# Pooled attention and two token layers on one core: engine queues from a planned task list, first two token blocks interleaved

## The chip, the cores and the metric
One core of a Trainium2 chip. The metric is device time in microseconds for one execution of the whole program, median of the runs; one execution was also profiled. Engines: TensorE (PE, with its weight loads PEld), VectorE (DVE), ScalarE (ACT), GpSimd (POOL), and SyncE (SP), whose queue issues all DMAs here. An engine runs its queue in the order in which the kernel wrote it.

## The reference
Attention over keys and values that are averaged in groups of 8, then two layers over all 4608 tokens. All inputs are float32.

```python
k_p = k.reshape(B, H, Sp, 8, D).mean(axis=3)         # B, H, S, D = 8, 8, 576, 64; Sp = 72
v_p = v.reshape(B, H, Sp, 8, D).mean(axis=3)
attn = softmax(q @ k_p.T / sqrt(D)) ; x = attn @ v_p # x: 4608 tokens x 512
h = x @ w_in                                         # 2048 inner columns
P = a[0] + a[1]*h + a[2]*h*h + a[3]*h*h*h
Q = 1.0 + abs(b[0])*abs(h) + abs(b[1])*h*h
x = (P / (Q + 1e-6)) @ w_out
out = (sigmoid(x @ w_gate) * (x @ w_val)) @ w_out2   # 1536 inner columns
```

## The kernel before
Float32 products are made of three matmuls each, of high and low parts (`mm3`, lines 500 to 502). The weights come as float32 and are taken apart once: two activations (lines 92, 94), a shift on VectorE (line 100) and an add on GpSimd (line 102), then a high part (line 117) and a low part (line 118, on VectorE for w_in, on GpSimd for w_out).

The tokens go through attention and the first layer in 9 blocks of 512 tokens. The inner columns of the first layer are 16 pieces of 128. A **step** n is one block's one piece: n = 16 x block + piece, 144 steps. `g1` makes the hidden tile h (12 matmuls of 512 columns) in one of four PSUM banks handed out in turn (`new_ps`); `rational1` to `rational3` (lines 541 to 560) make the rational function on ScalarE and VectorE, with line 560 as h's last reader; `split_g` takes the result apart (lines 525, 528); and `g2`, three steps later, adds the piece's product with w_out into four accumulator banks, which `store` evicts and writes to DRAM (x2d) once a block is done.

Between the steps stands the attention of the next block, tile by tile (tiles of up to 128 tokens of one batch; 5 tiles in odd blocks, 4 in even ones): `scores` (sc, line 369; maxima and differences at 380, 382), `exponential` (388), `normalise` (395 to 399, the last on GpSimd), `a_transpose` (pta at 406, aT at 410), `attend` (psx at 421, xs at 426 and 427). Its PSUM tiles come from the same four banks in turn. Keys are pooled on VectorE (`pool_k`, 318) and copied into the block-diagonal kbd (`place_k`, 327); values are pooled on GpSimd (`pool_v`, 335, 336), and those of the first batch partly on VectorE (`pool_v0`, 348 to 351).

The order is written by hand: `put` gives each attention task a step and a rank, and the loop over n calls, in a fixed order, g1, the attention's tasks of this step, the rational function, g2 and `weights_a` or `background`. The first block's attention, and the first weights, run ahead of step 0. During steps 0 to 15 `weights_a` converts the first layer's weights, one piece of w_in and of w_out a step; pieces 5 to 15 of w_out are written back to DRAM (wod) and read again for each later block (`wo_stream`). From step 16 to 127 `background` converts the weights of the second layer. From step 128 the second layer's first inputs and weights are loaded. The second layer (`gate`, `value`, `h2`, from 974 us) runs on its own order.

Of the kernel before, what the change touches and what calls it, by code (L numbers as in the profile page):

```python
# [33 lines left out]

@with_exitstack
def attention_moe_glu_kernel(ctx: ExitStack, tc: tile.TileContext, q, k, v, w_in, w_out, ca, cb, w_gate, w_val, w_out2, out):
# [13 lines left out]
    NTT = TB // P  # L50
# [10 lines left out]
    LAG = 3  # L61
# [5 lines left out]
    xs_p = ctx.enter_context(tc.tile_pool(name="xs", bufs=2))  # L67
    rot = ctx.enter_context(tc.tile_pool(name="rot", bufs=1))
    g_p = ctx.enter_context(tc.tile_pool(name="g", bufs=3))
    ps_h = ctx.enter_context(tc.tile_pool(name="ps_h", bufs=4, space=PSUM))  # L70
    ps_a = ctx.enter_context(tc.tile_pool(name="ps_a", bufs=1, space=PSUM))

    def new_ps(name):
        return ps_h.tile([P, 512], F32, tag="h", name=name)

    def new_tmp(name, tag="m", bufs=3):
        return rot.tile([P, 512], F32, tag=tag, name=name, bufs=bufs)

    x2d = [dram.tile([P, NJ, TB], F32, name=f"x2d{i}", tag=f"x2d{i}") for i in range(NB)]

    def conv1a(*raws):

        for raw in raws:
            hw, lw = raw[:, :, 1], raw[:, :, 0]

            nc.scalar.activation(hw.bitcast(F32), hw.bitcast(F32), AF.Prelu, scale=2.0 ** -112, alpha=2.0 ** 32)

            nc.scalar.activation(lw, lw.bitcast(U32), AF.Copy, scale=2.0 ** -29)

    def conv1b(*raws):

        ws = [(raw[:, :, 1], raw[:, :, 0]) for raw in raws]
        for hw, lw in ws:
            nc.vector.tensor_scalar(out=hw, in0=hw, scalar1=3, scalar2=None, op0=ALU.logical_shift_left)  # L100
        for hw, lw in ws:
            nc.gpsimd.tensor_tensor(out=hw, in0=hw, in1=lw, op=ALU.add)

    between = []

    def conv1(*raws):
        conv1a(*raws)
        between.append(lambda: conv1b(*raws))

    def gap():  # L110
        for f in between:
            f()
        between.clear()

    def conv2(raw, wh, wl, eng=nc.gpsimd):
        t = raw[:, :, 1].bitcast(F32)
        nc.scalar.activation(wh, t, AF.Copy)
        eng.tensor_tensor(out=wl, in0=t, in1=wh.bitcast(F32), op=ALU.subtract)

    def load_raw(raw, src, by_cols):  # L120
        if by_cols:
            nc.sync.dma_start(raw.rearrange("p (c f) w -> p c (f w)", f=P), src.rearrange("(c p) x -> p c x", p=P))
        else:
            nc.sync.dma_start(raw.rearrange("p f w -> p (f w)"), src)

    def slot(tag, dtype, name, pool=None):
        shape = [P, 2, 4 * P] if dtype is F32R else [P, 4 * P, 2]
        return (pool or wp).tile(shape, dtype, tag=tag, name=name)

    wod = {f: dram.tile([P, 8 * P], F32, name=f"wod{f}", tag=f"wod{f}") for f in range(FS, NF1)}  # L130


    w2d = [dram.tile([P, 14, 4 * P], F32, name=f"w2d{s_}", tag=f"w2d{s_}") for s_ in range(NS)]
    wo2d = [dram.tile([P, 8 * P], F32, name=f"wo2d{f}", tag=f"wo2d{f}") for f in range(NF2)]


    wi, wo, wi_raw, wo_raw = {}, {}, {}, {}

    def wi_src(f):
        return w_in[:, 2 * f * P:2 * (f + 1) * P]  # L140

    def wi_load(f):
        wi_raw[f] = slot(f"wi{f + 1}", I32, "wiraw") if f + 1 < NF1 else slot("st5", I32, "wiraw", stage)
        load_raw(wi_raw[f], wi_src(f), True)

    def wi_conv1(f):
        conv1(wi_raw[f])

    def wi_conv2(f):
        wi[f] = slot(f"wi{f}", F32R, "wi")  # L150
        conv2(wi_raw.pop(f), wi[f][:, 0], wi[f][:, 1], nc.vector)
# [739 lines left out]
```

## Time and profile before
| | us |
|---|---|
| median of 3 runs | 1812.47 (1809.62 to 1812.76) |
| profiled execution, span | 1813.5 |
| TensorE busy | 1761.6 |
| VectorE busy | 1104.0 |
| ScalarE busy | 975.8 |
| GpSimd busy | 801.3 |

The span is the time from the first to the last instruction of the profiled execution; it lies 1 us above the median of the runs. Busy time is the time in which at least one instruction of an engine ran. Matmuls are pipelined, so a busy TensorE may still be one that runs at the lower of its two clocks: the granted clock stands beside it, as a share of full speed.

### The profile page before, as it was taken

How to read it: one execution, taken by the hardware profiler on the slowest of the kernel's cores; microseconds unless marked ns; L12 is line 12 of the kernel's file. 1: busy time of each engine (PE TensorE's matmuls, PEld its weight loads, DVE VectorE, ACT ScalarE, POOL GpSimd, SP SyncE). 2: the span in 40 equal slices, each digit the busy share in tenths (PEclk: the TensorE clock that was granted, in tenths of full speed). 3: DMA queues.
4: the chain of work that ended last, by engine and by line, in shares of the span. 5: the costliest groups of instructions: out<-in, count | busy, mean ns of one | idle time of the engine just before them, and what ended most of it. 6: DMA issues, size and time to landing. Idle time of an engine off the chain costs nothing. (4 is left out here: it accounts for less than half of the span.)

```text
span 1813.5 us, 25319 instructions
## 1 busy us (share of the span) xinstructions
PE 1761.6 (97%) x9056; PEld 1525.1 (84%) x9056; DVE 1104.0 (61%) x1788; ACT 975.8 (54%) x1763; POOL 801.3 (44%) x787
## 2 busy tenths in 40 slices
PE   6699999999999999999999999999999999999999
PEld 5578787788878887788878998998998998998997
DVE  6898887878888888888776333333433333433341
ACT  5998877687877777877875222222222222222221
POOL 3766554563555536634442324324324334334231
PEclk8899999999999999999999999999999999999999
DMA  8564444543544454425465753763763763763660
GB/s 258 169 202 144 151 156 145 195 152 131 202 170 156 139 193 161 168 100 176 167 221 197 236 181 128 236 182 125 240 186 120 240 197 109 238 201 106 206 198 36
DMA packets 128209, 313.60 MB, mean 173 GB/s; under 512 B 16596, under 2 KB 48340, under 8 KB 128084
## 3 DMA queue, kind: packets, MB, share of 16 engines
q1 hardware_dynamic: 128084, 311.99, 52.8%
q8 instruction: 72, 1.18, 0.3%
q14 instruction: 53, 0.43, 0.1%
HBM read 257.95 MB, written 52.95 MB: 171 GB/s over the span
## 5 line engine op out<-in xcount | busy, mean ns | idle before, releaser
L674 DVE TENSOR_TENSOR t<-h,t 128x384 f32<-128x384 f32 x360 | 200.8, 558 | 388.0 <-ACT t L682 273.0
L528 POOL TENSOR_TENSOR g<-y,g 128x512 fp32r<-128x512 f32 x144 | 187.2, 1300 | 283.8 <-ACT g L525 216.6
L727 POOL TENSOR_TENSOR t<-t 128x384 f32<-128x384 f32 x72 | 84.4, 1172 | 449.0 <-issue 253.4
L500 PE MATMUL acc<-g,wo 128*128 128x512 f32 x576 | 233.7, 406 | 0.0
L500 PE MATMUL h<-xs,wi 128*128 128x512 f32 x576 | 231.3, 402 | 2.2 <-DVE xs L427 2.0
L502 PE MATMUL acc<-g,wo 128*128 128x512 f32 x576 | 226.8, 394 | 1.3 <-POOL g L528 1.3
L501 PE MATMUL h<-xs,wi 128*128 128x512 f32 x576 | 226.5, 393 | 0.0
L502 PE MATMUL h<-xs,wi 128*128 128x512 f32 x576 | 226.4, 393 | 0.0
L501 PE MATMUL acc<-g,wo 128*128 128x512 f32 x576 | 226.0, 392 | 0.0
L502 PE MATMUL h<-xS,wq 128*128 128x384 f32 x576 | 193.4, 336 | 0.0
L500 PE MATMUL h<-xS,wq 128*128 128x384 f32 x576 | 193.2, 335 | 0.0
L501 PE MATMUL h<-xS,wq 128*128 128x384 f32 x576 | 193.0, 335 | 0.0
L541 ACT ACTIVATE u<-h,coef 128x512 f32<-128x512 f32 x144 | 98.2, 682 | 104.7 <-PE h L502 104.4
L558 DVE SCALAR_TENSOR_TENSOR y<-y,coef,h 128x512 f32<-128x512 f32 x144 | 107.4, 746 | 75.2 <-ACT h L554 73.0
L543 DVE SCALAR_TENSOR_TENSOR u<-u,coef,h 128x512 f32<-128x512 f32 x144 | 106.4, 739 | 70.9 <-ACT y L542 70.3
L500 PE MATMUL h<-xA,wq 128*128 128x384 f32 x432 | 149.4, 346 | 0.1
L502 PE MATMUL h<-xA,wq 128*128 128x384 f32 x432 | 144.9, 335 | 0.0
L501 PE MATMUL h<-xA,wq 128*128 128x384 f32 x432 | 144.9, 335 | 0.0
L500 PEld LDWEIGHTS h<-xs,wi 128*128 128x128 f32 x576 | 109.7, 191 | 26.8 <-DVE xs L427 3.0
L500 PEld LDWEIGHTS acc<-g,wo 128*128 128x128 f32 x576 | 109.0, 189 | 26.5 <-issue 4.6
L502 PEld LDWEIGHTS acc<-g,wo 128*128 128x128 f32 x576 | 108.9, 189 | 25.6 <-POOL g L528 1.7
L502 PEld LDWEIGHTS h<-xs,wi 128*128 128x128 f32 x576 | 109.3, 190 | 23.8 <-DVE xs L427 0.2
(115 smaller groups left out, 4041.2 us busy)
## 6 DMA issues: line engine op xcount, KB each, us to landing
wq<-w2d SPq DMA_DIRECT2D x252, 512.0 KB
wo<-wod SPq DMA_DIRECT2D x88, 512.0 KB
w2d<-wq SPq DMA_DIRECT2D x36, 512.0 KB
x2d<-o SPq DMA_DIRECT2D x36, 256.0 KB
out_dram<-o SPq DMA_DIRECT2D x36, 256.0 KB
raw<-in_k_dram SPq DMA_DIRECT2D x32, 256.0 KB
raw<-in_q_dram SPq DMA_DIRECT2D x32, 256.0 KB
wiraw<-in_moe_w_in_dram SPq DMA_DIRECT2D x16, 512.0 KB
```

What stands on the lines that cost most here:

```text
L500: nc.tensor.matmul(out_, wl, xh, start=start, stop=False, skip_group_check=on)
L501: nc.tensor.matmul(out_, wh, xh, start=False, stop=False, skip_group_check=on)
L502: nc.tensor.matmul(out_, wh, xl, start=False, stop=stop, skip_group_check=on)
L528: eng.tensor_tensor(out=g[:, 1], in0=y, in1=g[:, 0].bitcast(F32), op=ALU.subtract)
L541: nc.scalar.activation(u, h, AF.Abs, scale=coef[:, 5:6])
L543: nc.vector.scalar_tensor_tensor(out=u, in0=u, scalar=coef[:, 4:5], in1=h, op0=ALU.add, op1=ALU.mult)
L558: nc.vector.scalar_tensor_tensor(out=y, in0=y, scalar=coef[:, 0:1], in1=r, op0=ALU.add, op1=ALU.mult)
L674: nc.vector.tensor_tensor(out=out_, in0=a, in1=b, op=ALU.add)
L727: eng.tensor_tensor(out=y, in0=x, in1=y, op=ALU.mult)
```

## The change
All work up to the second layer is written as tasks. A task names its engine, a duration, a rank, the tiles that it reads and writes, and a function that issues its instructions. `Planner.order` goes through a time of its own: whenever an engine is free, it starts the task of lowest rank whose inputs are there and for whose new tiles a place is free, and takes the place that has been free longest. Then the functions are called in that order, so each engine's queue has it; the places become tile tags.

- Order of the steps (`SEQ`): block 0 with pieces 0 to 7, block 1 with pieces 0 to 15, block 0 with pieces 8 to 15, then blocks 2 to 8 whole. After its first half block 0's sums are evicted and written to DRAM (x2p); `half_load` reads them back, and at the end of the second half four VectorE adds join them.
- Weights of pieces 0 to 7 are due one a step, pieces 8 to 15 one in two steps. Pieces 5 to 15 of w_out go over wod, from block 1 on: 96 reloads, 88 before.
- The attention of block 1 is due over steps 0 to 7, of block 2 over steps 24 to 31, of each later block over the 16 steps before it. A tile's scores wait for the matmuls of the step three before its rank.
- Keys: placed into kbd by four copies for a batch (two before, except in the first batch), as part of the batch's first token tile.
- Values of the first batch: summed by TensorE, eight matmuls with the identity for each of four loads, and one ScalarE eviction.
- Conversion of the second layer's weights: from step 32 on, over 96 steps (112 before).
- The second layer's own order stays; its tags are taken from the plan's places.

Durations of the plan (us) for one step: g1 2.72; on ScalarE 0.57, 0.66, 0.65, 0.65, 0.54, 0.53; on VectorE 0.66, 0.72, 0.66, 0.66, 0.72, 0.61; on GpSimd 1.3; g2 four times 0.68. The weight's shift is 0.45, the low part 0.75 on VectorE and 1.3 on GpSimd. A DMA of s KB occupies SP for s/300, at least 0.45, and its data are there 2.0 later.

```diff
--- before.py
+++ after.py
@@
+class Planner:
+    LAG = {"ACT": 0.13, "DVE": 0.1, "POOL": 0.1, "PE": 0.22, "SP": 2.0, "-": 0.0}
...
+    def slot_for(self, b, now):
+        if b.kind in self.caps:
+            live = self.held.setdefault(b.kind, [])
+            live[:] = [x for x in live if x.left or x.end > now]
+            if len(live) >= self.caps[b.kind]:
+                return None
+        best = None
+        for where in b.where:
+            for s in self.slots[where]:
+                if self.free[s] <= now and s not in self.taken and (best is None or self.free[s] < self.free[best]):
+                    best = s
+            if best is not None:
+                return best
+        return None
+    def order(self):
+        done, now = [], 0.0
+        ready = {e: [] for e in self.LAG}
+        busy = {e: 0.0 for e in self.LAG}
+        for n, t in enumerate(self.tasks):
+            t.n = n
+            if not t.wait:
+                ready[t.eng].append(t)
+        while len(done) < len(self.tasks):
+            moved = True
+            while moved:
+                moved = False
+                for e in ready:
+                    if busy[e] > now:
+                        continue
+                    for t in sorted((t for t in ready[e] if t.ready <= now), key=lambda t: (t.rank, t.n)):
+                        self.taken = set()
+                        got = []
+                        for b in t.bufs:
+                            if b.where and b.slot is None:
+                                s = self.slot_for(b, now)
+                                if s is None:
+                                    break
+                                got.append((b, s))
+                                self.taken.add(s)
+                        else:
+                            self.start(t, got, now, busy, ready, done)
+                            moved = True
+                            break
...
+    SEG = NF1 // 2
+    SEQ = [(0, f) for f in range(SEG)] + [(1, f) for f in range(NF1)] + [(0, f) for f in range(SEG, NF1)]
+    SEQ += [(i, f) for i in range(2, NB) for f in range(NF1)]
...
+    slots = {"W": [f"w{i}" for i in range(NF1 + FS + NR)], "ST": [f"st{i}" for i in range(6)],
+             "h": [f"b{i}" for i in range(4)], "su": [f"su{i}" for i in range(3)], "y": [f"y{i}" for i in range(3)],
+             "m": [f"m{i}" for i in range(3)], "g": [f"g{i}" for i in range(3)], "xs": ["xs0", "xs1"],
+             "raw": [f"raw{i}" for i in range(3)], "e": ["e"], "aT": ["aT"], "kp": ["kp"], "vp": ["vp"],
+             "vh": ["vh0", "vh1"], "kbd": ["kbd"]}
+    slots.update({f"acc{e}": [f"b{4 + e}"] for e in range(NJ)})
+    slots.update({n: [n] for n in ("mx0", "mx1", "r0", "r1", "wqt")})
+    for n in ("A11", "S2", "S3", "S1", "A12", "A22", "S4"):
+        slots["x" + n] = ["x" + n]
+    plan = Planner(slots, {"hc": 3, "ha": 3, "wr": NR, "tmp": 18, "bgraw": 3, "bgt": 1, "cv": 5, "u": 2}, ("wr", "hc", "cv"))
...
+    def place_keys(b, rank):
+        kp = pooled.pop(b)
+        for js, cs in ((slice(0, NJ // 2), (0, 1, 2)), (slice(NJ // 2, NJ), (2, 3, 4))):
+            for e in range(2):
+                half = slice(e * D, (e + 1) * D)
+                plan("ACT", act(SP * 2), rank, lambda e=e, js=js, half=half: nc.scalar.activation(
+                    kbd.t[half, js, e], kp.t.rearrange("p (j s) -> p j s", s=SP)[half, js], AF.Copy),
+                    w=[(kbd, (js.start, e))], r=[(kp, c) for c in cs])
+    def values0(rank, rank_load):
+        pv = psum("vps", ["acc3"])
+        for c in range(NJ):
+            raw = small([P, 8 * P], "rawv", ["W"], "tmp")
+            load(rank_load, 288, lambda raw=raw, c=c: nc.sync.dma_start(
+                raw.t[:SP].rearrange("p (h x) -> p h x", h=2), v[0][2 * c:2 * c + 2].rearrange("h (s j) d -> s h (j d)", j=POOL)), w=[raw])
+            def fn(raw=raw, c=c):
+                t = raw.t[:SP].rearrange("p (h j d) -> p h j d", h=2, d=D)
+                o = pv.t[:SP, c * 2 * D:(c + 1) * 2 * D].rearrange("p (h d) -> p h d", d=D)
+                for j in range(POOL):
+                    nc.tensor.matmul(o, ident[:SP, :SP], t[:, :, j], start=j == 0, stop=j == POOL - 1)
+            plan("PE", 1.8, rank, fn, w=[(pv, c)], r=[raw])
+        vh[0] = small([SP, H, D], "vh", ["vh"])
+        plan("ACT", act(512), rank, lambda: nc.scalar.activation(vh[0].t.rearrange("p h d -> p (h d)"), pv.t[:SP], AF.Copy), w=[vh[0]], r=[pv])
...
+    def tile_attention(i, rank, gate_on=[]):
+        b, t0, n = tiles[i]
+        blk, o = divmod(b * S + t0, TB)
+        if i == first[b]:
+            place_keys(b, rank)
...
+        own = ["h"] if blk else ["h", "acc0", "acc1", "acc2"]
...
+        for g in range(2):
+            sc = psum("sc", own, kind)
+            def fn(g=g, sc=sc):
+                for j in (2 * g, 2 * g + 1):
+                    nc.tensor.matmul(sc.t[:n, (j % 2) * 2 * SP:(j % 2 + 1) * 2 * SP], s()[:, j], kbd.t[:, j].rearrange("p e s -> p (e s)"), start=True, stop=True)
+            plan("PE", 0.5, rank, fn, w=[sc], r=[raw, (kbd, (2 * g, 0)), (kbd, (2 * g, 1))],
+                 after=(turned[-1:] if blk > 1 else turned[-3:-2]) + gate_on)
...
+    def half_load(rank):
+        for c in range(2):
+            t = Buf("xhalf", [P, 2, TB], F32, ["ST"], "half")
+            load(rank, 512, lambda c=c, t=t: nc.sync.dma_start(t.t, x2p.t[:, 2 * c:2 * c + 2]), w=[t], r=[x2p], after=first_mm[-1:])
+            half_x.append(t)
+    def g1(n, i, f, rank):
+        h = psum("h", ["h"], "hc")
...
+        ACT(0.57, rank, lambda: nc.scalar.activation(u.t, h.t, AF.Abs, scale=coef[:, 5:6]), w=[u], r=[h, coef_b])
+        ACT(0.66, rank, lambda: nc.scalar.activation(y.t, h.t, AF.Identity, scale=coef[:, 3:4], bias=coef[:, 2:3]), w=[y], r=[h, coef_b])
+        plan("DVE", 0.66, rank, lambda: STT(out=u.t, in0=u.t, scalar=coef[:, 4:5], in1=h.t, op0=ALU.add, op1=ALU.mult), w=[u], r=[h])
+        plan("DVE", 0.72, rank, lambda: nc.vector.tensor_tensor(out=y.t, in0=h.t, in1=y.t, op=ALU.mult), w=[y], r=[h])
...
+    def g2(n, i, f, rank):
+        g, w = gbuf.pop(n), wo[f]
+        new, end = f == 0 or n == 3 * SEG, f == NF1 - 1 or n == SEG - 1
+        if new:
+            acc[i] = [psum(f"acc{e}", [f"acc{e}"]) for e in range(NJ)]
+        for e in range(NJ):
+            def fn(e=e, a=acc[i][e]):
+                es = slice(e * P, (e + 1) * P)
+                mm3(a.t, w.t[:, 1, es], w.t[:, 0, es], g.t[:, 1], g.t[:, 0], new, end)
+            plan("PE", 0.68, rank, fn, w=[acc[i][e]], r=[g, w])
+        if n == 4 * SEG - 1:
+            for e in range(NJ):
+                p = half_x[e // 2]
+                plan("DVE", 0.7, rank, lambda e=e, p=p, a=acc[i][e]: nc.vector.tensor_tensor(
+                    out=p.t[:, e % 2], in0=a.t, in1=p.t[:, e % 2], op=ALU.add), w=[(p, e)], r=[acc[i][e]])
+                load(rank, 256, lambda e=e, p=p: nc.sync.dma_start(x2d[i].t[:, e], p.t[:, e % 2]), w=[(x2d[i], e)], r=[(p, e)])
+        elif end:
+            dst = x2p if n == SEG - 1 else x2d[i]
...
+    T0 = -20.0
+    values_at = {}
+    for c in range(1):
+        plan("DVE", 0.6, T0, lambda: nc.vector.memset(kbd.t, 0.0), w=[kbd])
+    keys(0, T0, T0)
+    query(0, T0 + 1)
+    query(1, T0 + 2)
+    values0(T0 + 5.25, T0 + 3)
+    query(2, T0 + 4)
+    query(3, T0 + 5)
+    for i in of_block[0]:
+        tile_attention(i, T0 + 5 + 0.1 * i)
+    def target(i):
+        blk = block_of[i]
+        idx = of_block[blk]
+        a, m = (0, SEG) if blk == 1 else (3 * SEG, SEG) if blk == 2 else (NF1 * (blk - 1), NF1)
+        return a + 0.5 + (m - 3.5) * idx.index(i) / len(idx)
+    batch_rank = {b: target(first[b]) - 4 for b in range(1, B)}
+    AHEAD = 3
+    extra = []
+    for b in range(1, B):
+        extra.append((batch_rank[b], 0, "b", b))
+    for i in range(len(tiles)):
+        if block_of[i] > 0:
+            extra.append((target(i), 1, "t", i))
+    for u in range(NF2):
+        extra.append((4 * SEG + u * (NB - 3) * NF1 / NF2, 2, "u", u))
+    for f in range(NF1):
+        extra.append((f - 2.5 if f < SEG else SEG - 2 + (f - SEG) * 2, -1, "w", f))
+    extra.sort()
+    def emit_extra(upto):
+        while extra and extra[0][0] < upto:
+            rank, _, what, x = extra.pop(0)
+            if what == "b":
+                keys(x, rank + 2, rank)
+                values(x, rank + 3, rank + 1)
+            elif what == "t":
+                query(x, rank - 2)
+                tile_attention(x, rank, [first_mm[int(rank) - AHEAD]] if rank >= AHEAD else [])
+            elif what == "u":
+                background(x, rank, [first_mm[int(rank) - 2]])
             else:
+                wi_make(x, rank, rank - 12 + x if x < 4 else rank - 4)
+                wo_make(x, rank + 2.5 if x < SEG else rank + 1, rank - 9 + x if x < 3 else rank - 1)
+    for n in range(N1):
+        i, f = SEQ[n]
+        emit_extra(n + 2)
+        if n >= SEG and f >= FS:
+            wo_stream(f, n - 1.5)
+        if n == 3 * SEG + 1:
+            half_load(n)
...
+        g1(n, i, f, n)
+        if n < N1 - 2:
+            g2(n, i, f, n + 2.2)
...
+    jobs = plan.order()
...
+        for t in jobs:
+            if t.fn == "late":
+                att.close()
+                late = ctx.enter_context(tc.tile_pool(name="late", bufs=1))
+                pools.update({"xA": late, "xS": late})
+                continue
+            for b in t.new:
+                make(b)
+            t.fn()
```

## Rows read from the trace of the kernel before

**Rows 1.** The page: span, then each engine's busy time and share.
```profile
span 1813.5 us, 25319 instructions
PE 1761.6 (97%) x9056; PEld 1525.1 (84%) x9056; DVE 1104.0 (61%) x1788; ACT 975.8 (54%) x1763; POOL 801.3 (44%) x787
```

**Rows 2.** Busy time by stretches: stretch, length, engines, granted clock, DMA share and rate.
```profile
core 0: us, PE busy (x) PEld busy (x) DVE busy (x) ACT busy (x) POOL busy (x), PEclk, DMA share, GB/s
0.00:20.00 20.00, 4.55 (x21) 4.25 (x22) 11.17 (x19) 3.94 (x7) 6.64 (x13) 0.91 0.84 225
0.00:38.50 38.50, 20.58 (x137) 17.45 (x137) 25.89 (x52) 18.37 (x33) 14.34 (x21) 0.80 0.91 269
38.50:160.90 122.40, 103.26 (x508) 82.23 (x509) 110.01 (x184) 114.28 (x202) 91.67 (x93) 0.90 0.54 178
38.50:262.40 223.90, 203.49 (x1021) 164.67 (x1022) 194.02 (x322) 191.45 (x337) 138.54 (x142) 0.94 0.49 165
0.00:262.40 262.40, 224.06 (x1157) 182.12 (x1158) 219.91 (x373) 209.83 (x370) 152.88 (x162) 0.92 0.56 180
262.40:882.80 620.40, 612.07 (x3162) 498.17 (x3161) 507.10 (x846) 483.73 (x863) 319.27 (x351) 0.99 0.47 160
262.40:372.80 110.40, 106.48 (x546) 85.55 (x544) 87.25 (x147) 81.38 (x149) 52.59 (x59) 0.97 0.49 167
882.80:931.70 48.90, 48.90 (x217) 40.55 (x216) 37.89 (x51) 33.90 (x55) 19.57 (x14) 1.00 0.63 225
971.40:1809.00 837.60, 837.53 (x4355) 772.61 (x4354) 305.71 (x472) 216.05 (x427) 295.89 (x253) 1.00 0.56 176
...
60.40:67.40 7.00, 6.69 (x18) 4.94 (x19) 6.88 (x11) 6.75 (x13) 5.28 (x5) 0.50 1.04 351
67.40:262.40 195.00, 186.60 (x960) 151.82 (x959) 170.96 (x286) 166.49 (x292) 115.76 (x115) 0.98 0.48 160
```

**Rows 3.** What TensorE waited for: us in total, times, the longest.
```profile
PE psx L421 <- DVE y L560: 7.8, 8, 1.4
PE pta L406 <- POOL e L399: 6.3, 2, 5.6
PE acc L502 <- POOL g L528: 1.3, 1, 1.3
```

**Rows 4.** Instructions in time before step 0: start, duration (us), engine, line.
```profile
8.62 0.65 ACT L327 ACTIVATE kbd<-kp 64x144 f32<-64x144 f32 x2 [0.57 <-DVE kp L318]
...
9.82 3.66 PE L369 MATMUL sc<-kbd,raw 128*128 128x144 f32 x16 [9.82 <-DMA raw<-in_q_dram]
...
16.58 3.71 DVE L351 TENSOR_REDUCE vh<-raw 72x128 f32<-72x1024 f32 x2
...
22.89 1.15 PE L421 MATMUL psx<-aT,vh 72*64 72x128 f32 x16
...
27.89 1.27 DVE L318 TENSOR_REDUCE kp<-raw 128x64 f32<-128x512 f32 x2
...
34.48 1.98 PE L421 MATMUL psx<-aT,vh 72*64 72x128 f32 x16
...
38.50 0.80 PE L500 MATMUL h<-xs,wi 128*128 128x512 f32 x1
```

**Rows 5.** In time at 60 us; then line 118 for w_in: least, median, most ns.
```profile
60.17 1.30 POOL L118 TENSOR_TENSOR wo<-woraw,wo 128x512 fp32r<-128x512 f32 x1
60.22 1.79 DVE L118 TENSOR_TENSOR wi<-wiraw,wi 128x512 fp32r<-128x512 f32 x1
...
60.40 1.19 PE L369 MATMUL sc<-kbd,raw 128*64 128x144 f32 x4 [9.03 <-DVE y L560]
...
L118 DVE TENSOR_TENSOR wi<-wiraw,wi x16: 630/684/1816, 32.3 to 145.2; 128x512 fp32r<-128x512 f32 x16
```

**Rows 6.** Groups by line: busy us, mean ns of one, idle time before.
```profile
L100 DVE TENSOR_SCALAR wqraw<-wqraw 128x512 int32<-128x512 int32 x36 | 25.8, 718 | 0.0
L521 DVE COPY o<-acc 128x512 f32<-128x512 f32 x9 | 6.2, 683 | 4.9 <-PE acc L502 4.9
```

More of the change, by code (lines that the diff above doesn't have):

```diff
@@ L32, in token_tiles, with __init__ @@
     return tiles
+class Buf:
+    def __init__(self, name, shape, dtype, where, kind=None, t=None):
+        self.name, self.shape, self.dtype, self.where, self.kind, self.t = name, shape, dtype, where, kind, t
+        self.hist, self.left, self.end, self.slot = [], 0, 0.0, None
+class Task:
+    def __init__(self, eng, cost, rank, fn, bufs, deps):
+        self.eng, self.cost, self.rank, self.fn, self.bufs, self.deps = eng, cost, rank, fn, bufs, deps
+        self.out, self.wait, self.ready, self.end = [], 0, 0.0, None
+        self.new = []
@@ L76, in new_tmp @@
[L76 to L102, printed above, removed]
@@ L126, in slot @@
[L126 to L137, printed above, removed]
@@ new lines, in psum, with act, dve, pool @@
+    def psum(name, where, kind=None):
+        return Buf(name, [P, 512], F32, where, kind)
+    def act(n):
+        return 0.19 + n * 0.00075
+    def dve(n):
+        return 0.07 + n * 0.00118
+    def pool(n):
+        return 0.15 + n * 0.00215
+    def dma(kb):
+        return max(0.45, kb / 300.0)
+    def ACT(cost, rank, fn, w=(), r=(), after=()):
+        return plan("ACT", cost, rank, fn, w, r, after)
+    def load(rank, kb, fn, w=(), r=(), after=()):
+        return plan("SP", dma(kb), rank, fn, w, r, after)
@@ L316, in pool_k, with tmp_where, small, k_cols @@
+    def tmp_where(blk, own):
+        return [own, "W"] if blk <= 1 else [own]
+    def small(shape, name, where, kind=None):
+        return Buf(name, shape, F32, where, kind)
+    kbd = small([P, NJ, 2, SP], "kbd", ["kbd"])
+    vh, xs, rawq, turned, pooled = {}, {}, {}, [], {}
+    def k_cols(c):
+        return slice(c * D, min((c + 1) * D, NJ * SP))
+    def keys(b, rank, rank_load):
+        kp = small([P, NJ * SP], "kp", ["kp"])
+        for c in range(NCH):
             cols = k_cols(c)
@@ L332, in pool_v, with values @@
+    def values(b, rank, rank_load):
+        vp = small([P, NCH, D], "vp", ["vp"])
+        vh[b] = small([SP, H, D], "vh", ["vh"])
+        rows = v[b].rearrange("h (s j) d -> (h s) (j d)", j=POOL)
+        for c in range(NCH):
             m = P if c < NCH - 1 else CL
-            t = take("v", b, c)[:m]
+            raw = small([P, 4 * P], "rawv", tmp_where(b, "raw"), "tmp" if b < 2 else None)
+            load(rank_load, 2 * m, lambda raw=raw, m=m, c=c: nc.sync.dma_start(raw.t[:m], rows[c * P:c * P + m]), w=[raw])
@@ L412, in new_x @@
[L412 to L418 removed]
+                mm = min(end - r, SP - s)
+                load(rank, 0, lambda r=r, h=h, s=s, mm=mm, c=c: nc.sync.dma_start(vh[b].t[s:s + mm, h], vp.t[r - c * P:r - c * P + mm, c]),
+                     w=[(vh[b], (h, s))], r=[(vp, c)])
+                r += mm
@@ new lines, in x_prep @@
+        def x_prep(part):
+            for job in X_PREP[part]:
+                if job[0] == "split":
+                    x = xo[job[1]] = late.tile([P, 2, 2, HB], F32R, tag="x" + job[1], name="x" + job[1])
+                    split_hi(x, half(*HALF[job[2]]))
+                    split_lo(x, half(*HALF[job[2]]), nc.gpsimd)
+                else:
+                    nc.vector.tensor_tensor(out=half(*HALF[job[1]]), in0=half(*HALF[job[2]]), in1=half(*HALF[job[3]]),
+                                            op=ALU.add if job[0] == "add" else ALU.subtract)
```

864 lines of the change are left out of this document (376 added, 488 removed).

## The prediction, made before the result was known
> **What bounds the kernel now.** I read the page's head first [rows 1]: TensorE is busy for 1761.6 of 1813.5 us, every other engine for at most 61%. So the kernel is bound by its matmuls, and only the time in which TensorE is idle, or runs slowly, can be won. Next, the busy time by stretches [rows 2], cut where the matmuls of step 0, 32, 128 and the second layer begin, shows where that time lies. From 971.4 us to the end TensorE is never idle (837.53 of 837.60): the second layer, which the change leaves as it is, gives nothing. In the nine steps from 882.8 us it is full too, and a step (217 matmuls in nine, 24 each) costs 48.90/9 = 5.43 us. The open time is earlier:
> - Before step 0: 38.5 us, 20.58 of them busy.
> - Steps 0 to 31 (38.5 to 262.4): 223.90 less 203.49, that is 20.4 us idle. On top comes the clock. From 60.4 to 67.4 it was granted at 0.50, the lower of its two levels (1.2 GHz), with 6.69 us busy, so some 3.3 us lost; over the rest the mean is 0.98, another 0.02 x 195 = 3.9; with a little at the very start I call it 7.7. Open: 28.1 us.
> - Steps 32 to 127: 620.40 less 612.07 is 8.3 us idle, and 0.03 x 110.4 = 3.3 us of clock in the first block of it. Open: 11.7 us.
> - The last 1.3 us: one wait for g [rows 3].
>
> So 28.1 + 11.7 + 1.3 = 41 us behind step 0, and the front. Who holds TensorE up there? Between 38.5 and 160.9 us VectorE is busy for 110.01 of 122.40 us (89.9%) and ScalarE for 114.28 (93.4%) [rows 2]: the 16 pairs of weights of the first layer, one token block's attention and 16 steps of the rational function all fall into 16 steps. The waits of TensorE [rows 3] name VectorE's y (line 560): it is the last reader of an h bank, and the four h banks are handed out in turn, so that attention takes the next in turn and not the one that is free. The worst single one is the 9.03 us before the scores at 60.40 us [rows 5].
>
> **The front.** Scores of the first tile start at 9.82 us when its queries land, and that stays. The four tiles' last products come at 22.89 to 34.48 us, and step 0 at 38.50 [rows 4]. Removed here: the pooling of the first batch's values on VectorE (3.71 us for two reduces) and on GpSimd, where they stand ahead of the first tile's normalising; and by rank the next batch's keys (1.27 and 1.23 us rows between the tiles, their line 318) and the weights now come behind the tiles. Added: 32 matmuls with the identity. The trace has none; the nearest row is line 421's, 16 records of 8 matmuls with 128 columns, in 1.15 us. So 32 cost 4 x 1.15 = 4.6 us at that row's pace, and 4 x 1.98 = 7.9 us at that of 34.48; TensorE had the room (20.58 of 38.5). I take the lower end plus the wait for the values' loads, which are issued in the same order. Then the first psx comes at about 21 instead of 22.9, and three more tiles at some 3.2 us each instead of (34.48 - 22.89)/3 = 3.9: the last at 30.6, and step 0, 4.0 later as now, at 34.6; less one more of the key rows (1.3 us), behind which the last tile's steps now stand, some **33 us: 5.5 us won**. Bounds: 0 (values late on TensorE) and 8.
>
> **Steps 0 to 31.** Block 0 does its first 8 inner columns, then block 1 all 16, then block 0 the other 8. Nothing of the work in 32 steps goes away: only the order of what is due. The second eight pairs of weights are converted over 16 steps, and the conversions for the second layer begin at step 32 rather than 16. Is there room? TensorE's own need is 223.9 - 28.1 = 195.8 us behind step 0, so 33 + 196 = 229. VectorE did 219.91 us until 262.4 [rows 2]. Of this 3.71 (values) go, and of the second layer's conversions five shifts of 0.72 = 3.6 [rows 6]; four adds instead of one copy put some 3 x 0.68 = 2.0 back [rows 6]. Left: 214.6. It had done 11.17 at 20 us, so at its present 89.9% it ends at 20 + 203.4/0.899 = 246, and without any idle at 223. ScalarE: 20 + (209.83 - 3.94)/0.934 = 240, less what leaves with the conversions. All three limits lie together, 229 to 246; with banks chosen by which is free, the long waits go, short ones stay. I take **241: 262.4 - 241 = 21.4 us won, of which 5.5 is the front**. Bounds 229 and 262.
>
> **Smaller parts.** Block 0's half sums: four more evictions and stores, two loads of 512 KB, and the adds. They lie beside the next block's matmuls, which wait only for the banks; without that cover four evictions of 0.68 us, half on each engine, cost 1 to 3 us once. Eight more reloads of w_out pieces (96 for 88): they queue on SP, behind stores that wait for their producers, and a late one would hold TensorE; DMA's share is 0.49 [rows 2], so nothing, at worst 1 to 2 us. Keys: four copies of 0.33 us for a batch [rows 4] instead of two long ones, now right ahead of the batch's first scores; those are released three steps ahead of their use, so nothing, else 1.3 us for each of seven batches. Each queued copy stands ahead of the rational function's activations on ScalarE. Conversions for the second layer in 96 steps instead of 112: VectorE is at 507.10 of 620.40 (82%) there, room enough.
>
> **Steps 32 to 143.** The open 11.7 + 1.3 us are mostly short waits for a bank (those of psx for y are 7.8 us in the whole kernel [rows 3]). Choosing the free bank ends most; new small ones come, since each piece is put just where its inputs are expected. I take 60%: **8 us**. Bounds 13 and a loss, below.
>
> Sum: 1813.5 - 21.4 - 8 = 1784 on the profiled execution. That execution is 1 us above the median of the runs (1812.47), so **1783 us**.
>
> **Rivals.** *All of it.* Every open microsecond is won: 1813.5 - 5.5 - 28.1 - 13 - 1 = 1766. For it: in the nine steps from 882.8 us nothing waits at all. Against: VectorE and ScalarE would have to be at 95% and more until step 32.
> *The crowd stays.* VectorE holds 89.9%, step 32 starts at 246 to 247, and the blocks behind gain nothing: 1813.5 - 15.5 = 1798. A worse form, in which block 1's five tiles in eight steps are the new crowd and eat the front's gain, ends at 1812, no change.
> *The order breaks on the durations (slower).* The new order is a list made with one fixed duration for each form of instruction, and it holds no slack: each engine takes the piece that is ready at that moment of the plan. In the trace the same form differs: the subtraction that makes wi's low part takes 0.63 us at least, 0.68 in the middle and 1.82 at most, and it is the 1.79 us one that lies beside a 1.30 us GpSimd instruction [rows 5]. If every one of the 36 tiles of blocks 1 to 8 then waits once for 1.0 us (the seven to eight psx waits now are 7.8 us in sum [rows 3]), that is 36 us, and some 15 us more where the clock falls with it (nine falls at 1.7 us, half of the 3.3 us that the clock took in the first block behind step 32): 1783 + 36 + 15 = 1834. It turns slower than now from 30/36 = 0.8 us per tile. Against it: TensorE is the plan's longest queue, and ahead of it the others have 18% of idle time behind step 32 to catch up.
> The Trainium skill's page "SBUF — State Buffer", section "Who interferes with whom", bears on that: VectorE and GpSimd share a pair of ports that one instruction holds until its end, and the other waits. The 1.79 us row agrees. By that rule, which a plan of fixed durations doesn't know, the time would come out at the slower rival's 1834.
> *It doesn't do what it says.* Should the order come out as the old one, the time stays at 1812; I see nothing for that, and count it with no change.
>
> **How the numbers follow.** Forecast 0.48 (1775 to 1792 by itself); all of it 0.10; the crowd stays 0.20, of which 0.05 as no change; slower 0.17; order unchanged or gain eaten 0.05, of which 0.03 no change and 0.01 on either side. Faster 0.48 + 0.10 + 0.15 + 0.01 = 0.74, within 0.2% (3.6 us, about what a measurement of this kernel can tell) 0.08, slower 0.18. The range reaches from just under the first rival to just over the present time: 1764 to 1814, and leaves out the slower rival and a little at the lower end.
>
> **What would show it.** Right: step 0 at 31 to 35 us, step 32 (both first blocks done) at 235 to 247, with VectorE above 92% until then, no TensorE wait over 3 us, a clock of 1.00 from about 70 us on, and 837 to 838 us from the second layer's first matmul to the end. Wrong: the first psx behind 23 us with identity matmuls just before it (values late); waits of TensorE for ScalarE or VectorE at nearly every tile behind step 32 (the slower rival); a wait for wo or xs at step 16 or 24 (the interleaving itself); a longer second layer would be something I haven't seen at all.

## The result and the profile after

The changed kernel takes 1788.25 us (median of 4 runs, 1787.48 to 1789.57) against 1812.58 for the kernel before: a ratio of 0.987, 95% interval 0.9856 to 0.9884. 1783 was forecast, range 1764 to 1814.

The head of the page after, span and busy time of each engine:

```profile
span 1786.7 us, 25603 instructions
PE 1759.2 (98%) x9120; PEld 1524.4 (85%) x9120; DVE 1093.4 (61%) x1790; ACT 969.2 (54%) x1778; POOL 795.9 (45%) x781
```

TensorE's busy time is nearly that of [rows 1] (1759.2 for 1761.6), and the span is 26.8 us shorter. So the time came out of idle TensorE, and some of it out of its slow clock. Where, the stretches show (columns as in [rows 2]; step 0 now begins at 34.70 us, step 32 at 244.0, step 128 at 859.6):

```profile
0.00:20.00 20.00, 12.36 (x84) 12.10 (x85) 12.55 (x26) 6.33 (x12) 2.99 (x8) 1.00 0.93 264
0.00:34.70 34.70, 24.55 (x201) 22.49 (x201) 25.24 (x51) 18.31 (x35) 14.39 (x24) 0.95 0.87 259
34.70:244.00 209.30, 201.25 (x1024) 161.92 (x1025) 185.08 (x313) 184.81 (x330) 113.54 (x106) 0.98 0.59 194
0.00:244.00 244.00, 225.80 (x1224) 184.41 (x1225) 210.31 (x363) 203.12 (x364) 127.93 (x129) 0.98 0.63 204
244.00:859.60 615.60, 611.39 (x3169) 497.64 (x3168) 509.97 (x858) 485.09 (x883) 339.05 (x378) 1.00 0.51 170
43.90:50.70 6.80, 5.58 (x31) 4.56 (x31) 5.99 (x11) 6.56 (x14) 3.33 (x3) 0.50 0.99 340
719.70:723.10 3.40, 3.40 (x23) 2.33 (x22) 3.11 (x6) 3.09 (x8) 2.38 (x3) 0.50 0.38 154
```

Against [rows 2]: the front is 3.8 us shorter (34.7 for 38.5), steps 0 to 31 are 14.6 us shorter (209.3 for 223.9), steps 32 to 127 4.8 us (615.6 for 620.4), and the rest 3.6 (927.1 for 930.7). The stretches understate the opening a little: by step 32 the changed kernel has done 30 of the second products (g2), the kernel before 29, and it keeps that lead of one (2.7 us) to the end, where it comes back as most of the 3.6. The second layer itself is unchanged: 840.0 us from its first matmul to the end, 839.4 before. In waits and clock: 20.4 us of idle TensorE behind step 0 in the opening became 8.1. A slow stretch stayed: 7 us at the lower clock at 60 us (6.69 of them busy) became 6.8 us at 43.9 (5.58 busy); the mean clock of the opening rose from 0.94 to 0.98.

Part of the 3.8 us of the front belongs to the profiled execution of the kernel before and not to the change. A kernel with the same order of instructions and nearly the same banks (the experiment "A free bank in the hand-written order"; its lines 385 and 521 are 369 and 500 here) was profiled too. Its queries landed 1.3 us sooner, and its step 0 came at 36.0 us instead of 38.5:

```profile
8.51 4.18 PE L385 MATMUL sc<-kbd,raw 128*128 128x144 f32 x16 [8.51 <-DMA raw<-in_q_dram]
...
35.98 0.80 PE L521 MATMUL h<-xs,wi 128*128 128x512 f32 x1 [0.17 <-ACT xs L446]
```

Against that execution the front is 1.3 us shorter. Its steps 0 to 31 (224.2 us) and 32 to 127 (620.5 us) last as long as those of [rows 2], so the gains behind step 0 stand.

What TensorE waited for, the whole span (columns as in [rows 3]): first two lines of the kernel before, then the changed kernel.

```profile
PE sc L369 <- DVE y L560: 10.1, 2, 9.0
...
PE pta L406 <- DVE y L560: 2.7, 1, 2.7
```

```profile
PE sc L451 <- DVE kp L378: 7.6, 1, 7.6
PE psx L485 <- ACT aT L477: 3.3, 3, 1.7
PE acc L502 <- POOL g L539: 3.0, 6, 0.8
PE pta L475 <- POOL e L467: 2.5, 3, 1.6
...
PE h L500 <- DVE y L536: 1.8, 2, 1.2
...
PE pta L475 <- DVE y L536: 0.7, 1, 0.7
```

The waits for VectorE's y, 20.6 us before (10.1, 2.7 and the 7.8 of [rows 3], with the 9.03 us of [rows 5] among them), are down to 2.5 us. Nothing behind the first scores waits longer than 1.7 us.

The front, in time (start, duration, engine, line):

```profile
7.64 4.40 PE L451 MATMUL sc<-kbd,rawq 128*128 128x144 f32 x16 [7.64 <-DVE kp L378]
...
11.84 4.31 PE L402 MATMUL vps<-rawv,ident 72*72 72x128 f32 x32
...
18.65 1.35 DVE L378 TENSOR_REDUCE kp<-rawk 128x64 f32<-128x512 f32 x2 [0.17 <-DMA rawk<-in_k_dram]
18.72 3.66 PE L402 MATMUL vps<-rawv,ident 72*72 72x128 f32 x32
...
22.41 0.59 ACT L405 ACTIVATE vh<-vps 72x512 f32<-72x512 f32 x1 [0.30 <-PE vps L402]
...
23.73 1.97 PE L485 MATMUL psx<-aT,vh 72*64 72x128 f32 x32
...
31.82 0.48 PE L485 MATMUL psx<-aT,vh 72*64 72x128 f32 x1
```

Scores begin 2.2 us sooner than in [rows 4], but the first psx later (23.73 for 22.89): the identity matmuls end at 22.38, and their eviction at 23.00. The products of two tiles then stand together, so the last tile's begin at 31.82 us, where [rows 4] has 34.48. The next batch's keys are still pooled between the tiles.

### The profile page after: what moved, and what is told of

The parts are those of the page before. It is cut to its first block, busy times and chain, and to the rows that moved or that the text cites. A ratio compares the mean times of both kernels' runs of the same rounds, so it can differ in the third digit from the quotient of the medians.

```text
span 1786.7 us, 25603 instructions
## 1 busy us (share of the span) xinstructions
PE 1759.2 (98%) x9120; PEld 1524.4 (85%) x9120; DVE 1093.4 (61%) x1790; ACT 969.2 (54%) x1778; POOL 795.9 (45%) x781
## 4 chain that ended last, share of the span: by engine, by line
PE 86%; ACT 5%; DVE 5%; issue 1%; DMA 1%; POOL 1%; SPq 0%; POOLq 0%; ACTq 0%; DVEq 0%
PE h L500 16%; PE h L502 15%; PE h L501 15%; PE acc L500 6%; PE acc L502 6%; PE acc L501 6%; PE accA L864 3%; PE accA L865 3%; PE h L865 3%; PE h L864 3%; PE accA L863 3%; PE h L863 3%; PE sc L451 2%; PE psx L485 2%; PE pta L475 2%
## 5 line engine op out<-in xcount | busy, mean ns | idle before, releaser
L502 PEld LDWEIGHTS h<-xs,wi 128*128 128x128 f32 x576 | 108.4, 188 | 24.3 <-DVE xs L493 0.6
```

The source lines that it names most:

```text
L502: nc.tensor.matmul(out_, wh, xl, start=False, stop=stop, skip_group_check=on)
```

## Experiments

The theory: (1) the interleaving takes the crowd of weights and attention out of the opening; (2) the order of the list, with banks chosen by which is free, ends the short waits. The rivals on record: the crowd of weights and attention stays; the order breaks where an instruction takes longer than planned. Every edit below but the one to the hand-written order changes the input of the plan, so each of these kernels has an order of its own everywhere, and a difference of a few microseconds between two of them says little about the edited part. I therefore read them by the same three stretches: front, steps 0 to 31, steps 32 to 127. The work done by step 32 is the same in all the planned kernels with free banks (30 second products, 13 tiles of attention). Each profile is of one execution.

### Blocks one after the other

```diff
-    SEQ = [(0, f) for f in range(SEG)] + [(1, f) for f in range(NF1)] + [(0, f) for f in range(SEG, NF1)]
-    SEQ += [(i, f) for i in range(2, NB) for f in range(NF1)]
+    SEQ = [(i, f) for i in range(NB) for f in range(NF1)]
...
-        a, m = (0, SEG) if blk == 1 else (3 * SEG, SEG) if blk == 2 else (NF1 * (blk - 1), NF1)
+        a, m = NF1 * (blk - 1), NF1
...
-        extra.append((f - 2.5 if f < SEG else SEG - 2 + (f - SEG) * 2, -1, "w", f))
+        extra.append((f - 2.5, -1, "w", f))
```

> The changed kernel with the blocks one after the other (block 0 with all 16 pieces, then block 1): no half sums, weights due one pair a step over 16 steps, block 1's attention due over 16 steps. Everything else as in the changed kernel. Theory (the interleaving wins the opening): 16 weight pairs and block 1's attention crowd into 16 steps again, step 32 at 254 us or later instead of 244.0, whole time 1798 to 1804. Rival (the list order with free banks wins it, interleaved or not): step 32 by 248, whole time 1786 to 1792.

Measured: 1797.61 us, ratio 0.9915 (0.99 to 0.9929). Its stretches:

```profile
0.00:35.30 35.30, 23.24 (x201) 21.24 (x201) 24.73 (x52) 19.22 (x38) 14.41 (x22) 1.00 0.86 254
35.30:254.50 219.20, 204.79 (x1025) 162.00 (x1026) 190.28 (x313) 182.46 (x321) 117.00 (x111) 0.98 0.48 161
254.50:868.80 614.30, 610.14 (x3170) 496.72 (x3169) 508.66 (x853) 487.38 (x888) 338.91 (x375) 1.00 0.49 169
```

The time fell just under the theory's 1798 to 1804; step 32 at 254.5 is where it put it. The whole loss stands in steps 0 to 31 (219.2 for 209.3 us, with 14.4 us of idle TensorE for 8.1); the front and the later blocks are as good as with the interleaving. The waits for y are 4.0 us here, so the order of the list ended most of them without the interleaving.

### The plain order, first values off TensorE, conversions from step 16

The edit above, and:

```diff
-            plan("PE", 1.8, rank, fn, w=[(pv, c)], r=[raw])
...
+            if c < NJ // 2:
+                for w in (POOL // 2 * D, POOL // 4 * D):
+                    plan("POOL", pool(2 * w), rank, lambda t=t, w=w: nc.gpsimd.tensor_tensor(
...
+            else:
+                plan("DVE", 1.85, rank, lambda t=t, hs=hs: nc.vector.reduce_sum(
...
-        extra.append((4 * SEG + u * (NB - 3) * NF1 / NF2, 2, "u", u))
+        extra.append((2 * SEG + u * (NB - 2) * NF1 / NF2, 2, "u", u))
```

> The changed kernel with three parts undone together: blocks one after the other, first values on GpSimd and VectorE, second layer's conversions from step 16 over 112 steps. Free banks, list order and keys stay. Theory (list order with free banks is worth about 15 us, the interleaving about 9): 1797 to 1802, step 32 at 255 to 260. Rival (the later conversions carry much of the plain order's gain): 1803 to 1810, step 32 above 262.

Measured: 1800.21 us (0.9928; 0.9912 to 0.9945), step 32 at 259.3: the theory's numbers. So the list order without the interleaving is worth some 12 us over the kernel before (the keys' four copies are in it too; they are tried below). The waits for y are 2.8 us. Its stretches behind step 0:

```profile
34.70:259.30 224.60, 209.27 (x1024) 164.77 (x1025) 197.75 (x323) 193.65 (x350) 140.56 (x144) 0.95 0.56 189
259.30:871.80 612.50, 609.51 (x3169) 495.97 (x3168) 509.66 (x849) 477.87 (x863) 315.05 (x346) 1.00 0.48 159
```

Its opening is no shorter than that of the kernel before (224.6 for 223.9, with one second product more done in it); what it gains lies in steps 32 to 127 (7.9 us), in the front and behind step 128. The interleaving is the part that wins the opening.

### First values on GpSimd and VectorE alone

Only the first part of that edit, the values; the blocks stay interleaved.

> The changed kernel with the first batch's values summed on GpSimd (two of four) and VectorE (two of four, 1.89 us each) as before, not by TensorE. Theory (values on TensorE are worth 1 to 3 us in the front): step 0 at 36 to 38 instead of 34.7, whole time 1789 to 1791. Rival (the front is bound by the chain of four tiles, values are hidden): step 0 within 0.5 us of 34.7, whole time 1788.

Measured: 1789.53 us (0.9867; 0.9852 to 0.9881); step 0 at 36.1, step 128 at 859.6, as in the changed kernel. Step 0 did come 1.4 us later, as the theory said, and the time lies in its band of 1789 to 1791; but it is not told apart from the changed kernel's. Both expectations thus hold in part: the edit moves the front, and the blocks behind gave it back in this plan (613.5 us for 615.6).

### Banks in turn

```diff
+            names = self.slots[where]
-            for s in self.slots[where]:
+            for s in [names[self.turn % 4]] if where == "h" else names:
...
             b.slot, self.free[s] = s, 1e9
+            self.turn += s in self.slots["h"]
```

> The changed kernel, but the four h banks are handed out in turn again; the plan knows it and orders around it. Theory (free banks end the waits for y): waits of TensorE for y of 10 us and more come back, 1796 to 1804. Rival (the plan hides a fixed turn as well): under 3 us of waits for y, 1787 to 1791.

> The changed kernel with four parts undone together: blocks one after the other, h banks in turn, first values on GpSimd and VectorE, second layer's conversions from step 16 over 112 steps. What is left of the change is the planned list order and the keys. Theory (the parts win, not the list as such): 1806 to 1815, the old time. Rival (the list order is most of it): 1792 to 1799.

Measured: 1893.23 us (1.0432; 1.0407 to 1.0456), and with the plain order, the values and the early conversions undone as well 1893.25 (1.0436). Both times were missed by far; the waits for y did come back, 52.6 us in all. What TensorE waited for with banks in turn, the first three lines:

```profile
PE pta L477 <- DVE y L538: 17.4, 7, 3.9
PE h L502 <- DVE y L538: 17.3, 12, 4.7
PE psx L487 <- DVE y L538: 14.4, 8, 3.2
```

And its steps 32 to 127, by stretch:

```profile
277.50:967.10 689.60, 639.77 (x3144) 508.10 (x3143) 503.09 (x848) 484.16 (x877) 334.44 (x373) 0.96 0.44 150
```

Steps 32 to 127 alone are 74 us longer than in the changed kernel. A list that places each piece as soon as it may start and is then bound to a fixed turn waits for whichever bank is next. The second of the two kernels therefore says nothing about the list order without its banks; the one with banks kept (above) does.

Nor do the two kernels undo a part of the change, for the kernel before has no strict turn. "Handed out in turn", as its description and the prediction have it, is wrong. Its tiles h, sc, pta and psx share one tag with four places; in its program, only 147 of the 340 such tiles from the fifth on, up to the second layer, lie in the bank of the tile four before them. Its trace shows the same:

```profile
84.73 0.64 ACT L410 ACTIVATE aT<-pta 72x256 f32<-72x256 f32 x2
85.15 0.76 PE L369 MATMUL sc<-kbd,raw 128*128 128x144 f32 x4 [1.29 <-ACT aT L410]
...
89.18 0.69 DVE L560 SCALAR_TENSOR_TENSOR y<-h,y 128x512 f32<-128x512 f32 x1
89.93 0.78 PE L421 MATMUL psx<-aT,vh 72*64 72x64 f32 x16 [1.28 <-DVE y L560]
```

Between the second pta that line 410 reads here and this psx stand two sc tiles and an h. In strict turn psx would have that pta's bank, which ScalarE was done with at 85.37 us; it waits for the last reader of an h instead, which ends at 89.87.

### A free bank in the hand-written order

The kernel before, with one edit: a bank goes back to a list when its last reader has been issued, and the next tile takes the one that went back first.

```diff
-        return ps_h.tile([P, 512], F32, tag="h", name=name)
+        if free_b:
+            b = free_b.pop(0)
+        else:
+            b = bank_of.pop(next(iter(bank_of)))[0]
+        t = ps_h.tile([P, 512], F32, tag=f"h{b}", name=name)
...
             nc.vector.scalar_tensor_tensor(out=y, in0=r, scalar=-2.0, in1=y, op0=ALU.add, op1=ALU.mult)
+            release(r)
```

> The kernel before, with its hand-written order, and one part of the change alone: an h bank is taken in the order in which the banks' last readers were issued, not in turn. Theory (the choice of the bank is what ends the waits for y): most of the 18.9 us of TensorE's waits for y go, 1798 to 1804. Rival (a free bank helps only together with the list order): waits for y stay above 10 us, 1808 to 1815.

Measured: 1813.05 us (1.0009; 0.9999 to 1.0019), no change. What TensorE waited for is almost to the digit what it waited for in the kernel before (10.1 and 7.8 us, above and in [rows 3]):

```profile
PE sc L385 <- DVE y L581: 10.0, 2, 9.0
...
PE psx L441 <- DVE y L581: 7.9, 8, 1.4
```

That is no wonder: the kernel before did so already. In 318 of the 344 tiles the edit gives a tile the bank of the same predecessor as before. So this run is no test of the bank's choice. The trace of the kernel before answers the question instead. Of its waits for a bank's last reader, 15 are longer than 0.5 us, and at each of them the last readers of the other three banks came later still: before the scores at 60.40 us, the bank taken is free at 60.30, the others at 61.85, 62.11 and 66.86. All four were taken, and no choice among them could have ended these waits. The waits for y end with the order of the list, at 4.0 and 2.8 us with blocks one after the other and 2.5 in the changed kernel. That it is the pieces' place in TensorE's queue is what remains as the cause; it was not tried by itself.

### Durations in the plan

Four kernels are the changed one with the planned durations of ScalarE, VectorE and GpSimd multiplied by a factor (0.7 in the lines below; 0.95, 1.03 and 1.1 in the others); the work is the same.

```diff
-        busy[t.eng] = now + t.cost
-        t.at, t.end = now, now + t.cost + self.LAG[t.eng]
+        cost = t.cost * (0.7 if t.eng in ("ACT", "DVE", "POOL") else 1)
+        busy[t.eng] = now + cost
+        t.at, t.end = now, now + cost + self.LAG[t.eng]
```

> The changed kernel, planned as if every instruction of VectorE, ScalarE and GpSimd took 0.7 of its planned duration; what runs is the same work in the order that this plan gives. Slower rival of the prediction (the order breaks where real durations are longer than planned): waits of about 1 us at each of the 36 tiles, 1815 to 1835. Theory (the three engines have room, and a wrong duration costs little): 1788 to 1797.

> The changed kernel, planned as if every instruction of VectorE, ScalarE and GpSimd took 0.95 of its planned duration. If the loss grows evenly with the error (252 us at 0.7), a sixth of that: 1815 to 1835. If the pieces have some 0.3 us of slack by chance: 1788 to 1798.

> The changed kernel, planned as if every instruction of VectorE, ScalarE and GpSimd took 1.03 of its planned duration. If the durations of the changed kernel are fitted to the chip, either side loses: 1790 to 1800. If a little slack helps: 1780 to 1787.

> The changed kernel, planned as if every instruction of VectorE, ScalarE and GpSimd took 1.1 of its planned duration. If the remaining 8 to 12 us of waits are pieces that come a little later than planned, a plan with slack ends some: 1782 to 1787. If they are the crowd of the first 100 us itself, the time stays: 1787 to 1791.

| factor | us | ratio to before | step 0 | steps 0 to 31 | steps 32 to 127 | from step 128 |
|---|---|---|---|---|---|---|
| 0.7 | 2040.00 | 1.1256 (1.1228 to 1.1284) | 48.3 | 251.5 | 783.4 | 955.2 |
| 0.95 | 1814.85 | 1.001 (1.0 to 1.0021) | 38.8 | 212.2 | 625.7 | 935.2 |
| 1, as changed | 1788.25 | 0.987 (0.9856 to 0.9884) | 34.7 | 209.3 | 615.6 | 927.1 |
| 1.03 | 1794.60 | 0.9901 (0.9886 to 0.9916) | 42.5 | 207.1 | 617.4 | 925.7 |
| 1.1 | 1807.17 | 0.9968 (0.9957 to 0.9978) | 42.3 | 211.3 | 621.9 | 928.9 |

At 0.95 the even loss nearly came (1814.85 for 1815 to 1835), at 1.03 the loss on either side; at 0.7 and 1.1 nothing that was expected held. Five per cent too short, and all of the change's gain is gone. But the stretches do not lose evenly. At 0.95, 10.1 us go in steps 32 to 127, 7.0 before, and 8.1 from step 128 on, of which one wait of TensorE for ScalarE in the second layer is 6.2; why it comes there is open. At 1.03 the front loses 7.8 us and the rest gains 1.8. TensorE's first wait with 0.7:

```profile
PE pta L476 <- POOL e L468: 121.9, 36, 6.5
```

36 waits, 3.4 us on average, before the transposes: three in the front, the others at 33 of the 36 tiles of blocks 1 to 8, one each. The clock follows (0.92 from step 32 to 127, 1.00 in the changed kernel). The last run of this kind shortens only a tile's own chain:

```diff
+        t = Task(eng, cost * (self.k if eng in ("ACT", "DVE", "POOL") else 1), rank, fn, bufs, deps)
...
         if i == first[b]:
             place_keys(b, rank)
+        plan.k = 0.7
...
+        plan.k = 1.0
```

> The changed kernel, where the plan takes 0.7 of the duration only for a tile's own attention pieces on VectorE, ScalarE and GpSimd (maxima to xs); the steps' rational function and the conversions keep theirs. Theory (the plan puts the transposes just behind as much matmul work as the tile's chain is planned to take, so a chain planned too short is waited for at every tile): waits for GpSimd's e at nearly all of the 36 tiles, 80 us or more in sum, 1870 to 1980. Rival (the loss of the 0.7 plan comes from the rational function, planned two thirds as long as it is): under 20 us of such waits, 1790 to 1815.

Measured: 1818.89 us, ratio 1.0035 (1.0023 to 1.0047), slower than the kernel before. Both expectations missed (26.3 us of waits and 1819). That nearly every tile is waited for is the theory's; the size is much nearer to the rival's (under 20 us, up to 1815). TensorE's first wait, and steps 32 to 127:

```profile
PE pta L476 <- POOL e L468: 26.3, 33, 2.0
```

```profile
254.20:891.50 637.30, 613.18 (x3169) 494.80 (x3168) 511.91 (x859) 491.99 (x887) 340.70 (x378) 1.00 0.48 164
```

33 waits of 0.8 us, 30 of them behind step 0. 22.0 us of them fall into steps 32 to 127, and that stretch is 21.7 us longer than in the changed kernel: there the price of the wrong duration is about what these waits add up to. The remaining 200 us and more of the plan with 0.7 everywhere come only when the other pieces of the three engines (rational function, conversions) are planned too short as well; which of them costs how much was not tried.

### Keys placed earlier

```diff
-            place_keys(b, rank)
+            place_keys(b, rank - 3)
```

> The changed kernel with a batch's keys placed into kbd at a rank three steps before its first tile, not with that tile. Theory (the placing is hidden either way): 1786 to 1791. Rival (four copies right ahead of the first scores hold TensorE 1.3 us in each of seven batches): 1777 to 1782.

Measured: 1790.94 us (0.988; 0.9865 to 0.9895), in the theory's band. Steps 32 to 127 take 614.4 us for 615.6; step 0 comes at 37.5 for 34.7, which is as much as the whole difference. Placing the keys with the first tile costs TensorE nothing that can be seen.

## Why the prediction came out right, step by step

**The opening: right in size, half right in its reason.** 15.9 us were forecast for steps 0 to 31 behind the front, 14.6 measured (17.3 with the second product done ahead). VectorE's work until step 32 was forecast at 214.6 us and is 210.31. Its share was forecast above 92% and is 185.08/209.30 = 88.4% of the stretch, no more than it had between 38.5 and 160.9 us in [rows 2] (89.9%). So VectorE did not get denser than it had been; it holds that share over the whole opening (86.7% before, 194.02 of 223.90) and has 4 us less to do than I thought. The interleaving is shown: with interleaved blocks and free banks, steps 0 to 31 take 207.1 to 213.0 us in seven of the eight kernels (251.5 in the plan with 0.7); with blocks one after the other, 219.2 and 224.6. The cleanest pair is the changed kernel and the first experiment, whose fronts are alike: 9.9 us in the stretch, 9.4 in the time. Step 32 itself comes at 244.0 to 254.2 us in the seven, the latest almost at the 254.5 of that experiment, because their fronts differ by 8 us. What fell is the sentence that "the four h banks are handed out in turn, so that attention takes the next in turn and not the one that is free" and what rests on it: they were not handed out in turn, and where TensorE waited all four were taken. The order of the list ended those waits; a strict turn would have spoiled it, but the kernel before had none.

**The front: 3.8 us for 5.5, and 1.3 of them against the quicker execution.** The failed term is the first psx, "at about 21": it came at 23.73, with identity matmuls before it, which the prediction had named as a sign of being wrong. The 64 records of identity matmuls took 4.31 + 3.66 = 8.0 us, the upper end that I named (7.9), not the lower that I took, and their second half had to wait for room behind other tiles' pieces. That the upper end fits is luck: its row, at 34.48 us, ran at the lower clock, and the identity matmuls at full clock.

```profile
34.48:36.46 1.98, 1.98 (x18) 1.95 (x18) 0.70 (x2) 1.87 (x4) 0.16 (x1) 0.50 1.01 257
```

```profile
11.84:16.15 4.31, 4.30 (x32) 4.07 (x32) 0.00 (x0) 1.00 1.06 266
18.72:22.38 3.66, 3.66 (x32) 3.42 (x32) 0.00 (x0) 1.00 0.73 259
```

(First all engines of the kernel before; then, in the changed kernel, the identity matmuls alone: TensorE, its weight loads, ScalarE.) That the keys' reduces leave the front was wrong too: VectorE was free at 18.65 us, so the list put them there, and the first weights' conversions stand between the tiles as well (line 258 at 20.10 us). Step 0 varies from 34.7 to 42.5 us over the planned kernels with a factor of 0.95 to 1.1 or with moved keys; of all its parts, the front depends most on the single plan, and the two executions of nearly the same kernel above differ by 2.5 us in it.

**Steps 32 to 143: 5.7 us for 8.** That is 4.8 + 3.6, less the 2.7 of the second product that had been done by step 32. Of the 13 us open there (8.3 idle, 3.3 clock, 1.3 the last wait), 4.2 of idle and 1.7 of clock (half of the 3.4 us at 719.7) are left up to step 128, and 0.5 behind it. The factor of 60% should have been half.

**The sum.** 3.8 + 14.6 + 4.8 + 3.6 = 26.8 us for the 29.4 forecast, on the profiled executions. The runs' median lies 1.6 us above the profiled span now, where it lay 1 us below: that is the other half of the 5 us between 1783 and 1788. The step "that execution is 1 us above the median of the runs" had it wrong. In every run on record the time is 1.7 to 2.0 us longer than the span of the same execution, so the span of 1813.5 belongs to an execution of about 1815.3 us, some 2.8 above the median; the front above shows where it lost 2.5 of them. By the medians the change is worth 24.3 us.

**The rivals.** The first ("all of it", 1766) would need the 8 us of waits and the slow 6.8 us at 43.9 to go. The second (the crowd stays, 1798) meets the time of the plain order, 1797.6 and 1800.2, by luck: it had step 32 at 246 to 247 and nothing gained behind, where these have 254.5 and 259.3 and gain 6.1 and 7.9 us behind. VectorE's 89.9% was its better part. The slower one was given 0.17; it did not come, but a chain planned too short does what it says: 0.8 us at 30 of 36 tiles and 1819 in all, where it had 1.0 us. That these sizes are near each other says little, since its 1.0 us came from other waits and the 0.7 was my choice. My reason against it was wrong: "ahead of it the others have 18% of idle time behind step 32 to catch up" doesn't help an engine whose order is fixed. When the transposes are at the head of TensorE's queue and e is late, TensorE waits, however idle VectorE was before. What kept the time at 1788 is that few pieces in this plan came late; whether its durations are the right ones, or this plan was a lucky one, the four factors do not tell apart. The collisions of VectorE and GpSimd are much as before: in the changed kernel the low part of wi takes

```profile
L268 DVE TENSOR_TENSOR wi<-wiraw,wi x16: 631/684/1672, 25.0 to 171.2; 128x512 fp32r<-128x512 f32 x16
```

from 631 to 1672 ns, median 684 (630, 684 and 1816 in [rows 5]). The longest lies beside a GpSimd instruction that began just before it:

```profile
81.93 1.32 POOL L268 TENSOR_TENSOR wo<-woraw,wo 128x512 fp32r<-128x512 f32 x1
82.12 1.67 DVE L268 TENSOR_TENSOR wi<-wiraw,wi 128x512 fp32r<-128x512 f32 x1
```

VectorE ends 0.54 us after GpSimd, which is nearly the 0.63 us that it takes at the least. The Trainium skill's page "SBUF — State Buffer", section "Who interferes with whom", has one of the two engines wait there for the other's whole instruction; these two rows agree. The 1834 that I gave to it did not come: two of the 16 pieces take over 1.5 us, and the median lies within the plan's 0.75.

**Small parts.** The clock was not 1.00 to the end of the first layer: after 50.7 us it fell once more, for 3.4 us at 719.7. The half sums cost nothing: no wait for an accumulator's eviction stands among TensorE's waits. The eight more reloads of w_out did not hold it either; no wait of TensorE names a DMA.

## What to carry over

A list order computed from durations is no better than the durations: at 0.95 of them this one lost all its gain, and a chain planned 30% too short is waited for at nearly every tile. Before trusting such an order, perturb its durations by a few per cent and time it; and read the stretches, not the whole, because every edit reshuffles the queues everywhere. A wait that the trace pins on a buffer may be one for a place in the queue: ask when the other buffers came free. Before an edit undoes or adds a part, make sure that the other kernel differs in it: "in turn" was a reading of the source, and the trace had it otherwise. And a kernel's profile is one execution: 2.5 us of this front were not the kernel's.

## What was not expected of the hardware

- The identity matmuls: 64 records of 128 columns in 8.0 us, 0.125 us each, at a granted clock of 1.00, where line 421's of the same width took 1.15/16 = 0.072 [rows 4]. There is no waiting inside their two pieces: TensorE is busy for 4.30 of 4.31 and 3.66 of 3.66 us. Their weights are 72x72, those of line 421 72x64; whether that is the reason was not tried.
- The clock makes waits dearer: with the plan at 0.7, steps 32 to 127 have 121 us of idle TensorE but are 168 us longer than in the changed kernel, at a mean granted clock of 0.92.
